# Causal attention with beacon tokens and a three-way maxout FFN on one core: the opening's loads, casts, masks and weight requests in another order

## The chip, the core and the metric

The kernel runs on one core of a Trainium2 chip. The core has a matrix engine (TensorE, "PE" in the profile, with its weight loads as "PEld"), VectorE ("DVE"), ScalarE ("ACT"), GpSimd ("POOL") and SyncE ("SP"), and 16 DMA engines that bring data from the chip's memory. Each engine runs its own list of instructions strictly in order, and waits at an instruction until what that instruction needs is there. The metric is the device time of one execution in microseconds. The program below is planned by hand: the order in which it is written is the order on each engine.

## The reference

Inputs are float32: `q`, `k`, `v` of shape 8 x 8 x 576 x 64 (batches, heads, tokens, width), 16 beacon keys and values for each head, three FFN matrices of 512 x 768 and one of 768 x 512.

```python
k_all = np.concatenate([beacon_k, k], axis=2)
v_all = np.concatenate([beacon_v, v], axis=2)
scores = scale * np.matmul(q, k_all.transpose(0, 1, 3, 2))
causal = np.zeros((S, Nb + S), dtype=bool)
causal[:, Nb:] = np.triu(np.ones((S, S), dtype=bool), k=1)
scores = np.where(causal, -1000000000.0, scores)
a = np.exp(scores - scores.max(-1, keepdims=True))
a /= a.sum(-1, keepdims=True) + 1e-09
attn = np.matmul(a, v_all)
x = attn.transpose(0, 2, 1, 3).reshape(B * S, H * D)
h = np.maximum(np.maximum(x @ w1, x @ w2), x @ w3)
out = h @ w_out
```

Every token sees the 16 beacons and the tokens up to itself. The output is 4608 x 512.

## The kernel before

**Units of work.** A *pair* is two heads of one batch; there are 32 pairs, four to a batch. For a pair, queries and keys are loaded in float32 (`load_pair`, L161), cast to bf16 (`cast_pair`, L192, with `cast_piece`, lines 181 and 186), turned on TensorE so that the head's width lies on partitions (`turn`, L297: `turn_apart` L337 early, `turn_pair` L344 later), and copied from the matrix engine's accumulators into `qT` and `kT` (L321, L332). The pair's beacon keys are copied into the first 16 columns of `kT` by `place_beacons` (L328). Then `emit_scores` (L375) makes the scores of a pair in four *groups* of key tiles (L385) and ScalarE takes their exponential (L394) into `at_sb`. `emit_masks` (L398) zeroes what lies above the diagonal: five small pieces for each pair, on VectorE by a product with a triangle (L408) for pairs 0 to 3, on GpSimd by a select (L410) for all later ones. `emit_pv` (L430) multiplies with a column of ones and with the values (L451), for a *quad* of two pairs and a half of the tokens at a time; `finish_pv` (L462) divides by the sums (L469, L471, L474) and writes `xT`.

**Values** of a batch come as five tiles of up to 128 tokens and all heads, in two pieces of three and two tiles (`load_v`, L199: DMA lines 208 and 213), and are cast by `cast_v` (L217, line 229). Neighbouring tiles with the same number of rows are cast by one instruction, so that tiles 1 and 2 go with tile 0. Values are read from memory in runs of 64 floats, 256 bytes; pairs from number 4 on in runs of 1536 bytes.

**FFN.** `mm1_unit` (L497) multiplies 512 tokens with one 128-column part of w1, w2 or w3, and VectorE keeps the maximum (L505, L507); `mm2_unit` (L514) does the output. The matrices are asked for on GpSimd's DMA queue (`load_w`, L238, two requests for each; `load_w_out`, L243), which casts on the way.

**Order.** `emit_all` (L671) goes through pairs `p` and steps `s`. Pairs 0 to 4 have four steps, one for each group ("fine" steps); later pairs have two. At a step TensorE gets the scores, then the work of `fine_at` (early turns, early value products, dummy products `keep_busy` that only keep the matrix engine occupied), then masks, then the value products of `pv_at`, then FFN units up to an allowance that grows with the steps, the next pair's turn, and what `plan` holds for that step. The value products of quad 2, the first of batch 1, stand at step (6, 0), behind that step's scores and ahead of its FFN units. The first FFN units stand at step (4, 3).

`plan` is filled by `at_step` (lines 618 to 638): casts on GpSimd and requests for weights. `C(...)` is a cast followed by `next_load()`, which issues the next entry of the list `loads` (lines 567 to 573) on SyncE's queue; `L(...)` is a call alone. SyncE's DMAs use eight semaphores in turn, so the ninth waits for the first to land, and a load into `st` waits for a free one of nine buffers. In the opening SyncE runs well ahead of what has been used.

Of the kernel before, what the change touches and what calls it, by code (L numbers as in the profile page):

```python
# [16 lines left out]
def kernel(  # L17
# [19 lines left out]
    d_model, d_ff = moe_w1.shape  # L37
# [19 lines left out]
    k_rows = [min(128, NK - 128 * t) for t in range(n_kt)]  # L57
# [9 lines left out]
    B_PE = 4  # L67
# [8 lines left out]
    NG = len(groups)  # L76
# [34 lines left out]
    bk16_1 = const.tile([NB_PE - Nb, H, D], BF16, name="bk16_1")  # L111
# [36 lines left out]
    by_pool = nc.gpsimd.tensor_copy  # L148
# [68 lines left out]
    def cast_v(b, piece, cast):  # L217
        st = stage.pop(("v", b, piece))
        if b not in v_tiles:
            v_tiles[b] = v_pool.tile([128, n_kt, H, D], BF16, name="v_sb")  # L220
        v_sb = v_tiles[b]
        t_lo, t_hi = V_PIECES[piece]
        t = t_lo
        while t < t_hi:
            t1 = t + 1
            while t1 < t_hi and k_rows[t1] == k_rows[t]:
                t1 += 1
            n = k_rows[t]
            cast(  # L229
                v_sb[0:n, t:t1].rearrange("p t h d -> p (t h d)"),  # L230
                st[0:n, (t - t_lo) * H * D : (t1 - t_lo) * H * D],
            )
            t = t1
# [92 lines left out]
    def place_beacons(p, copy):  # L326
        b, pi = divmod(p, PPB)
        copy(kTs[p % NT][:, 0:Nb], bT[:, pi, Nb * b : Nb * (b + 1)])  # L328
# [15 lines left out]
    def turn_pair(p, q_copy):  # L344
        banks = [pv_bank(i, [128, 1024], BF16) for i in range(2)]
        for i in range(2):
            turn(p, i, banks[i][:, 0:S])
        evac_q(p, banks[0][:, 0:S], q_copy)
        evac_k(p, banks[1][:, 0:S], by_dve)
# [25 lines left out]
    def emit_scores(p, gi):  # L375
        if gi == 0:
            at[p] = at_pool.tile([128, AT_W], BF16, name="at_sb")
        kT = kTs[p % NT]
        qT = qTs[p % NT]
        ps = sc_psum.tile([128, 2, 512], FP32, name="sc")  # L380
        off = 0
        for t, q0, q1 in groups[gi]:
            for e in range(2):
                hs = slice(64 * e, 64 * e + 64)
                nc.tensor.matmul(  # L385
                    ps[:, e, off : off + q1 - q0],
                    kT[hs, 128 * t : 128 * t + 128],
                    qT[hs, q0:q1],
                    start=True,
                    stop=True,  # L390
                    tile_position=(64 * e, 0),
                )
            off += q1 - q0
        nc.scalar.activation(  # L394
            out=both_heads(p, gi), in_=ps[:, :, 0 : g_width[gi]], func=AF.Exp, scale=scale
        )
# [146 lines left out]
    def emit_ffn(limit, pool=None, name="fps"):  # L543
        if done[0] + 1 <= limit and done[0] < len(units) and units[done[0]][0] <= ready[0]:
            _, fn, args = units[done[0]]
            fn(*args, pool or ffn_psum, name)
            done[0] += 1
            return True
        return False
# [5 lines left out]
    def at_step(p, g, *fns):  # L555
        plan.setdefault((p, g), []).extend(fns)

    def L(fn, *a):
        return lambda: fn(*a)

    def load_v_pieces(b):
        return [L(load_v, b, 0), L(load_v, b, 1)]

    def load_pairs(p0, p1):
        return [L(load_pair, p) for p in range(p0, p1)]

    loads = [L(load_pair, 0, nc.scalar), L(load_pair, 1, nc.scalar)] + load_pairs(2, 4)
    loads += [L(load_v, 0, 0), L(load_beacons, 1, B_PE, bk32_1), L(load_v, 0, 1)]
    loads += load_pairs(4, 5) + load_pairs(5, 6) + load_v_pieces(1) + load_pairs(6, 8)
    for b in range(2, B):  # L570
        if b == B_PE:
            loads.append(L(load_beacons, B_PE, B, bk32))
# [2 lines left out]
    def next_load(n=1):  # L575
        for _ in range(n):
            if loads:
                loads.pop(0)()

    def C(fn, *a):  # L580
        def run():
            fn(*a)
            next_load()

        return run

    def start():
        keep_busy(15)
        next_load()
        load_beacons(0, 1, bk32_0, nc.scalar)  # L590
        next_load(10)
        cast_piece(0, 0, by_dve)
        cast_piece(0, 1, by_act)
        stage.pop(("pair", 0))
        by_pool(bk16_0, bk32_0)
        next_load()
        q_ps = ffn_psum.tile([128, S], BF16, name="fps")
        k_ps = ffn_psum.tile([128, S], BF16, name="fps")
        turn(0, 0, q_ps)
        turn(0, 1, k_ps)  # L600
        evac_q(0, q_ps, by_act)
        evac_k(0, k_ps, by_dve)
        turn_beacons(0, 1, bk16_0)
        keep_busy(4)
        C(cast_pair, 1, by_pool, by_pool)()
# [9 lines left out]
    def steps(p):  # L615
        return [[gi] for gi in range(NG)] if p < P_FINE else [[0, 1], [2, 3]]

    at_step(0, 0, C(cast_pair, 2, by_pool, by_pool))
    at_step(0, 1, C(cast_pair, 3, by_pool, by_pool))
    at_step(1, 0, C(cast_v, 0, 0, by_pool))  # L620
    at_step(1, 1, C(cast_v, 0, 1, by_pool))
    at_step(1, 2, L(by_pool, bk16_1, bk32_1))
    at_step(1, 3, L(load_w, 0, 0, d_ff))
    at_step(2, 0, C(cast_pair, 4, by_pool, by_pool))
    at_step(2, 2, C(cast_pair, 5, by_pool, by_pool))
    at_step(3, 1, L(load_w, 1, 0, d_ff))
    at_step(3, 2, C(cast_v, 1, 0, by_pool))
    at_step(3, 3, C(cast_v, 1, 1, by_pool))
    at_step(4, 0, C(cast_pair, 6, by_pool, by_pool))
    at_step(4, 2, L(load_w, 2, 0, d_ff))  # L630
    at_step(4, 3, C(cast_pair, 7, by_pool, by_pool))
    at_step(5, 1, L(load_w_out))
    for p in range(8, B_PE * PPB):
        at_step(p - 2, 1, C(cast_pair, p, by_pool, by_pool))
    for b in range(2, B):
        p = b * PPB
# [7 lines left out]
        (0, 3): [L(turn_apart, 2, 1)],  # L644
        (1, 0): [L(turn_apart, 3, 0)],
        (1, 1): [L(turn_apart, 3, 1)],
        (1, 2): [L(keep_busy, 1, 256, True)],
        (1, 3): [L(keep_busy, 1, 256, True)],
        (2, 0): [L(emit_pv, 0, 0, 0, 2)],
        (2, 1): [L(emit_pv, 0, 0, 2, 4), finish_pv],  # L650
        (2, 2): [L(keep_busy, 1, 256, True)],
        (2, 3): [L(turn_beacons, 1, B_PE, bk16_1), L(keep_busy, 2, 256, True)],
        (3, 0): [L(turn_apart, 4, 0)],
        (3, 1): [L(turn_apart, 4, 1), L(emit_pv, 0, 1, 0, 2)],
        (3, 2): [L(emit_pv, 0, 1, 2, 4), finish_pv],
# [7 lines left out]
    for b in range(B_PE, B):  # L663
        p = b * PPB
# [6 lines left out]
    def emit_all():  # L671
        start()
        n_step = 0
        n_y = 0
        for p in range(NPAIR):
            b, pi = divmod(p, PPB)
            fine = p < P_FINE
            for s, gs in enumerate(steps(p)):
                for gi in gs:
                    emit_scores(p, gi)  # L680
                for fn in fine_at.pop((p, s), ()):
                    fn()
                for gi in gs:
                    emit_masks(p, gi, p < PPB)
                for args in pv_at.pop((p, s), ()):
                    emit_pv(*args)
                if fine:
                    allowed = 2 if (p, s) == (P_FINE - 1, NG - 1) else 0
                else:
                    n_step += 1  # L690
                    if n_step <= 9:
                        allowed = 2 + n_step * (UPB - 2) / 9
                    else:
                        allowed = (n_step - 1) * UPB / (2 * PPB)
                if not fine and s == 0 and p + 1 < B_PE * PPB:
                    place_beacons(p + 1, by_pool)
                emit_ffn(allowed)
                if not fine and s == 1 and p + 1 < B_PE * PPB:
                    turn_pair(p + 1, by_act)
                store_y(n_y)  # L700
                n_y = len(y_out)
                for fn in plan.pop((p, s), ()):
                    fn()
                emit_ffn(allowed)
                n_y = len(y_out)
                if not fine:
                    finish_pv()
                while emit_ffn(allowed):
                    pass
            if pi == 1 and b > 0:  # L710
                v_tiles.pop(b - 1)
        assert not plan and not loads and not pv_at
        for hf in range(2):
            emit_ffn(len(units))
            emit_ffn(len(units))
            emit_pv(NPAIR // 2 - 1, hf)
            finish_pv()
        store_y(len(y_out))
        alone[0] = True
        i = 0  # L720
        tail = [(ffn_psum, "fps"), (sc_psum, "sc")]
        while emit_ffn(len(units), *tail[i % 2]):
            i += 1
            store_y(len(y_out))

    with tc.manual_schedule():
        emit_all()
# [30 lines left out]
```

## Time and profile before

| What | Value |
|---|---|
| Five runs, median (lowest to highest) | 305.67 us (304.89 to 306.51) |
| The profiled execution, its own time | 303.82 us |
| Span of its instructions | 302.1 us |
| TensorE busy | 286.9 us, 95% of the span |
| VectorE, ScalarE, GpSimd busy | 174.5, 143.3, 127.1 us |
| Mean granted TensorE clock | 0.983 of full speed |
| Chain that ended last | TensorE 81%, DMA 6%, SyncE's queue 5%, GpSimd 2% |
| Landing of a pair's query load (288 KB), median | 5.3 us after its issue |
| Landing of a weight request (384 KB in bf16), median | 9.2 us after its issue |

The profile cuts the span into 40 slices and gives a busy tenth for each; "PEclk" is the share of full speed that TensorE was granted. An instruction group names its line in the kernel, the engine, and what it writes and reads (out<-in). A wait is put down to what ended it. "POOL v_sb L229 <- DMA st<-in_v_dram" reads: GpSimd, at the cast of values in line 229, waited for the load of values.

### The profile page before, as it was taken

The numbers are of one execution on the slowest core, as the hardware profiler recorded it, in microseconds if no ns is written. First come the engines' busy times: TensorE is split into PE (matmuls) and PEld (weight loads), VectorE is DVE, ScalarE is ACT, GpSimd is POOL, SyncE is SP. The second block draws the span as 40 slices with busy tenths as digits, with TensorE's granted clock in tenths as the row PEclk, the third lists the DMA queues.
The fourth block names the chain that finished last, engine by engine and source line by source line (L and its number), as shares of the span: only waits on it lengthen the run. The fifth ranks groups of instructions, "written<-read, shape, count | busy, mean of one in ns | idle before, by whom it ended". The sixth has DMA issues, their size and how long they took to land.

```text
span 302.1 us, 8614 instructions
## 1 busy us (share of the span) xinstructions
PE 286.9 (95%) x3560; PEld 148.9 (49%) x3560; DVE 174.5 (58%) x335; ACT 143.3 (47%) x220; POOL 127.1 (42%) x254
## 2 busy tenths in 40 slices
PE   7888849999999999999999999999999999999995
PEld 4545324554455555454445687545454544444442
DVE  2876525656666466646564656465736575275373
ACT  3877625573555464636463546455645531400300
POOL 3591594455667566455445544562243210000000
PEclk9959988999999999999999999999999999999999
DMA  7999999999699799999999998657402001102003
GB/s 262 220 225 213 230 252 247 215 242 213 181 308 205 221 262 235 175 194 266 283 202 182 258 263 143 119 142 197 101 36 106 2 0 72 72 0 112 28 2 139
DMA packets 83095, 51.55 MB, mean 171 GB/s; under 512 B 62064, under 2 KB 76656, under 8 KB 83056
## 3 DMA queue, kind: packets, MB, share of 16 engines
q1 hardware_dynamic: 80976, 47.23, 68.5%
q0 software_dynamic: 1648, 3.15, 5.5%
q8 instruction: 28, 0.46, 0.7%
q10 hardware_dynamic: 432, 0.62, 0.6%
q14 instruction: 11, 0.09, 0.1%
HBM read 35.13 MB, written 14.22 MB: 163 GB/s over the span
## 4 chain that ended last, share of the span: by engine, by line
PE 81%; DMA 6%; SPq 5%; POOL 2%; DVE 2%; issue 1%; ACT 0%; DVEq 0%
PE fps L497 41%; PE fps L514 13%; PE pv L451 11%; PE sc L385 8%; PE sc L497 5%; DMA st<-in_v_dram 4%; SPq L213 3%; PE sc L514 2%; DMA st<-in_q_dram 2%; PE pv L301 1%; SPq L249 1%; DVE kT L332 1%; POOL p L186 1%; POOL at_sb L410 1%; SPq L172 1%
## 5 line engine op out<-in xcount | busy, mean ns | idle before, releaser
L394 ACT ACTIVATE at_sb<-sc 128x992 bf16<-128x992 f32 (+3 forms) x128 | 103.6, 861 | 102.4 <-PE sc L385 102.2
L497 PE MATMUL fps<-xT,w_sb 128*128 128x512 bf16 (+1 forms) x648 | 140.2, 357 | 0.6 <-DVE xT L474 0.6
L497 PEld LDWEIGHTS <-w_sb 128*128 128x128 bf16 x720 | 65.8, 98 | 71.0 <-issue 14.9
L507 DVE TENSOR_TENSOR hT<-hT,fps 128x512 bf16<-128x512 bf16 x96 | 65.7, 685 | 45.3 <-PE fps L497 45.1
L410 POOL TENSOR_SCALAR_AFFINE_SELECT at_sb<-at_sb 128x256 bf16<-128x256 bf16 (+2 forms) x140 | 51.0, 383 | 95.8 <-ACT at_sb L394 94.4
L186 POOL CAST p<-st 96x768 bf16<-96x768 f32 x56 | 44.8, 827 | 2.6 <-DMA q_dram<-p 2.5
L514 PE MATMUL fps<-w_out_sb,hT 128*128 128x512 bf16 x180 | 41.8, 379 | 0.0
L385 PE MATMUL sc<-qT,kT 64*128 64x288 bf16 (+4 forms) x384 | 36.4, 288 | 4.5 <-POOL kT L328 3.4
L505 DVE CAST hT<-fps 128x512 bf16<-128x512 f32 x42 | 29.0, 690 | 19.9 <-PE fps L497 19.8
L522 DVE COPY y<-fps 128x512 f32<-128x512 f32 x30 | 20.7, 689 | 27.9 <-PE fps L514 27.9
L514 PEld LDWEIGHTS <-hT 128*128 128x128 bf16 x216 | 20.5, 98 | 25.0 <-DVE hT L507 1.3
L474 DVE TENSOR_TENSOR xT<-pv,recip 128x288 bf16<-128x288 f32 (+2 forms) x93 | 27.2, 348 | 6.2 <-ACT recip L471 4.4
L451 PE MATMUL pv<-at_sb,v_sb 128*32 128x192 bf16 (+4 forms) x1352 | 28.9, 232 | 0.0
L385 PEld LDWEIGHTS <-kT 64*128 64x128 bf16 x384 | 13.8, 95 | 29.4 <-issue 18.8
L229 POOL CAST v_sb<-st 128x1536 bf16<-128x1536 f32 (+2 forms) x24 | 21.5, 912 | 13.8 <-DMA st<-in_v_dram 13.7
L451 PEld LDWEIGHTS <-v_sb 128*32 128x32 bf16 (+1 forms) x1408 | 25.0, 98 | 2.6 <-issue 1.3
L451 PE MATMUL pv<-at_sb,ones 128*32 128x288 bf16 (+4 forms) x492 | 18.1, 263 | 1.4 <-DVE at_sb L408 0.8
L497 PE MATMUL sc<-xT,w_sb 128*128 128x512 bf16 x72 | 18.5, 379 | 0.0
L469 ACT ACTIVATE lnd<-pv 128x288 f32<-128x288 f32 x31 | 12.9, 416 | 5.8 <-PE pv L451 5.8
L451 PEld LDWEIGHTS <-ones 128*32 128x32 bf16 (+1 forms) x512 | 11.1, 97 | 8.8 <-issue 6.0
L507 DVE TENSOR_TENSOR hT<-hT,sc 128x512 bf16<-128x512 bf16 x12 | 8.2, 687 | 12.5 <-PE sc L497 12.3
L505 ACT CAST hT<-sc 128x512 bf16<-128x512 f32 x6 | 3.5, 585 | 23.7 <-PE sc L497 23.7
(47 smaller groups left out, 116.7 us busy)
## 6 DMA issues: line engine op xcount, KB each, us to landing
st<-in_q_dram SPq DMA_DIRECT2D x32, 288.0 KB, 5.3
out_dram<-y SPq DMA_DIRECT2D x36, 256.0 KB, 2.8
st<-in_k_dram SPq DMA_DIRECT2D x30, 288.0 KB, 5.5
st<-in_v_dram SPq DMA_DIRECT2D x24, 256.0 KB, 6.2
w_sb<-in_moe_w_dram POOLq DMA_DIRECT2D x6, 384.0 KB, 9.2
q_dram<-p SPq DMA_DIRECT2D x16, 144.0 KB, 2.5
k_dram<-p SPq DMA_DIRECT2D x16, 144.0 KB, 2.7
st<-in_v_dram SPq DMA_DIRECT2D x8, 224.0 KB, 6.1
```

The lines of the kernel that those rows point to most:

```text
L186: cast(t16.rearrange("p r h d -> p h r d"), st[0:QP, i * NQ2 : (i + 1) * NQ2].rearrange("p (h r d) -> p h r d", h=2, r=QR),)
L229: cast(v_sb[0:n, t:t1].rearrange("p t h d -> p (t h d)"), st[0:n, (t - t_lo) * H * D : (t1 - t_lo) * H * D],)
L385: nc.tensor.matmul(ps[:, e, off : off + q1 - q0], kT[hs, 128 * t : 128 * t + 128], qT[hs, q0:q1], start=True, stop=True, tile_position=(64 ...
L394: nc.scalar.activation(out=both_heads(p, gi), in_=ps[:, :, 0 : g_width[gi]], func=AF.Exp, scale=scale)
L410: nc.gpsimd.affine_select(out=view, in_=view, compare_op=ALU.is_ge, fill=0.0, base=x0, pattern=[[0, 2], [1, hi - lo]], channel_multiplier=-1,)
L451: nc.tensor.matmul(ps[bank][32 * j : 32 * j + 32, lo + q0 - qa : lo + qb - qa], lhsT, at_view(PPQ * quad + j // 2, t, j % 2, q0, qb), star ...
L474: nc.vector.tensor_mul(xT[:, 2 * g + part - 1, c0 + ca : c0 + cb], ps[bank][:, lo : lo + cb - ca], recip[:, ca:cb],)
L497: nc.tensor.matmul(ps[:, o0 : o0 + n], w_in[i][:, ct, 128 * ft : 128 * (ft + 1)], xT[:, ct, x0 : x0 + n], start=(ct == 0), stop=(ct == n_c ...
L505: (by_act if alone[0] else by_dve)(hT[:, ft, :], ps)
L507: nc.vector.tensor_max(hT[:, ft, :], hT[:, ft, :], ps)
L514: nc.tensor.matmul(ps, hT[:, ft, 128 * tt : 128 * (tt + 1)], w_out_sb[:, ft, :], start=(ft == 0), stop=(ft == n_ft - 1),)
L522: nc.vector.tensor_copy(y, ps)
```

## The change

The value casts of batch 0 are made for each tile alone. Pair 6 is loaded ahead of batch 1's values. Pair 0's masks are taken from VectorE and put on GpSimd, behind the casts of pairs 1 to 3 and ahead of the first values' casts. Pair 4's casts go ahead of the first weight request, pair 6's ahead of the second; batch 1's value casts, pair 7's casts and the requests for the third and the output matrix move to later steps. Four calls of dummy products get two products of 320 columns in place of one or two of 256.

```diff
@@ cast_v
-            while t1 < t_hi and k_rows[t1] == k_rows[t]:
+            while b > 0 and t1 < t_hi and k_rows[t1] == k_rows[t]:
@@ loads
-    loads += load_pairs(4, 5) + load_pairs(5, 6) + load_v_pieces(1) + load_pairs(6, 8)
+    loads += load_pairs(4, 7) + load_v_pieces(1) + load_pairs(7, 8)
@@ plan
     at_step(0, 1, C(cast_pair, 3, by_pool, by_pool))
+    at_step(1, 0, *[L(emit_masks, 0, gi) for gi in range(NG)])
     at_step(1, 0, C(cast_v, 0, 0, by_pool))
     at_step(1, 1, C(cast_v, 0, 1, by_pool))
     at_step(1, 2, L(by_pool, bk16_1, bk32_1))
-    at_step(1, 3, L(load_w, 0, 0, d_ff))
-    at_step(2, 0, C(cast_pair, 4, by_pool, by_pool))
+    at_step(1, 3, C(cast_pair, 4, by_pool, by_pool))
+    at_step(2, 0, L(load_w, 0, 0, d_ff))
     at_step(2, 2, C(cast_pair, 5, by_pool, by_pool))
-    at_step(3, 1, L(load_w, 1, 0, d_ff))
-    at_step(3, 2, C(cast_v, 1, 0, by_pool))
-    at_step(3, 3, C(cast_v, 1, 1, by_pool))
-    at_step(4, 0, C(cast_pair, 6, by_pool, by_pool))
-    at_step(4, 2, L(load_w, 2, 0, d_ff))
-    at_step(4, 3, C(cast_pair, 7, by_pool, by_pool))
-    at_step(5, 1, L(load_w_out))
+    at_step(3, 2, C(cast_pair, 6, by_pool, by_pool))
+    at_step(3, 3, L(load_w, 1, 0, d_ff))
+    at_step(4, 1, C(cast_v, 1, 0, by_pool))
+    at_step(4, 2, C(cast_v, 1, 1, by_pool))
+    at_step(5, 0, L(load_w, 2, 0, d_ff))
+    at_step(5, 0, C(cast_pair, 7, by_pool, by_pool))
+    at_step(6, 0, L(load_w_out))
@@ fine_at
-        (1, 2): [L(keep_busy, 1, 256, True)],
-        (1, 3): [L(keep_busy, 1, 256, True)],
+        (1, 2): [L(keep_busy, 2, 320, True)],
+        (1, 3): [L(keep_busy, 2, 320, True)],
-        (2, 2): [L(keep_busy, 1, 256, True)],
-        (2, 3): [L(turn_beacons, 1, B_PE, bk16_1), L(keep_busy, 2, 256, True)],
+        (2, 2): [L(keep_busy, 2, 320, True)],
+        (2, 3): [L(turn_beacons, 1, B_PE, bk16_1), L(keep_busy, 2, 320, True)],
@@ emit_all
-                for gi in gs:
+                for gi in gs if p > 0 else ():
                     emit_masks(p, gi, p < PPB)
```

On GpSimd the list around step (6, 0) is now: first three of pair 4's masks, values of batch 1 (first piece), a mask, values (second piece), pair 4's last mask, pair 5's first three masks, pair 6's beacons, third weights, casts of pair 7, pair 5's last two masks.

## The prediction
> **What bounds the kernel now.** I read the page's slices first, because the change touches only the opening.
>
> ```profile
> PE   7888849999999999999999999999999999999995
> POOL 3591594455667566455445544562243210000000
> PEclk9959988999999999999999999999999999999999
> DMA  7999999999699799999999998657402001102003
> ```
>
> A slice is 7.55 us. From slice 7 (about 53 us) TensorE is 90% busy or more at full clock, in an order fixed by the program: whatever is won or lost before that moves the end by as much, and nothing later has room to give it back. The dips are slice 3 (clock) and slices 5 and 6 (TensorE idle, then clock). The DMA row is full throughout: the opening is a queue for bytes. The waits of the first 50 us name the dip in slice 5:
>
> ```profile
> POOL v_sb L229 <- DMA st<-in_v_dram: 13.7, 3, 9.9
> PE sc L385 <- POOL kT L328: 3.4, 1, 3.4
> ```
>
> The columns are total, times and longest. TensorE waits once, for 3.42 us, for a 16-column copy on POOL that was ready long before; POOL itself had waited 9.91 us for batch 1's values. The timeline from 31 us shows what stood between:
>
> ```profile
> 33.80 2.71 POOL L229 CAST v_sb<-st 128x1536 bf16<-128x1536 f32 x3 [9.91 <-DMA st<-in_v_dram]
> ...
> 37.16 1.58 POOL L186 CAST p<-st 96x768 bf16<-96x768 f32 x2
> ...
> 39.33 1.08 POOL L238 DMA_DIRECT2D w_sb<-in_moe_w_dram  x2
> ...
> 40.76 1.60 POOL L186 CAST p<-st 96x768 bf16<-96x768 f32 x2
> ...
> 42.31 1.01 POOL L410 TENSOR_SCALAR_AFFINE_SELECT at_sb<-at_sb 128x224 bf16<-128x224 bf16 x3
> ...
> 43.27 0.19 POOL L328 COPY kT<-bT 128x16 bf16<-128x16 bf16 x1
> 43.41 0.75 POOL L410 TENSOR_SCALAR_AFFINE_SELECT at_sb<-at_sb 128x256 bf16<-128x256 bf16 x2
> 43.51 0.74 PE L385 MATMUL sc<-qT,kT 64*128 64x288 bf16 x8 [3.42 <-POOL kT L328]
> ...
> 44.19 0.62 PE L451 MATMUL pv<-at_sb,ones 128*32 128x288 bf16 x12
> ```
>
> Columns: start, length, work. From 33.80 POOL never rests. Two things follow one another on it: pair 6's beacons at 43.27 release the scores of step (6, 0), and pair 5's last mask, done at 44.17, releases the value products at 44.19. TensorE had finished everything else at 40.10, and 1.23 us of that were waits for POOL's cast of pair 6 (0.89 + 0.34), so it could have been there at 38.9. **The stage is bound by DMA, then by POOL, with some 5 us of slack on TensorE.** Why batch 1's values came late is in the trace's packets: from 23 to 31 us the weights' queue moved about 30 packets of 3 KB in each 0.5 us and the load queue about as many of 256 B. Turns are by packet, so the values got under a tenth of the bytes until two weight matrices were in.
>
> **The change, part by part.** Working forward in the profiled execution (303.82 us, span 302.1).
>
> *Masks of pair 0 to POOL.* DVE loses five multiplies of 0.23 to 0.28 us, 1.3 us. POOL gains five selects of 0.32 to 0.40 (rows at 42.31 and 43.41), 1.8 us, from 10.7 to 12.5, where it idled 3.40 us for the values. The Trainium skill speaks against such a move (SBUF — State Buffer, "Who interferes with whom": a GpSimd instruction holds the port pair that it shares with VectorE to its end). The row: DVE's 16-column copy takes 0.15 us alone and 1.08 at 14.50, beside POOL's 1.47 us cast; but DVE's 576-column copies take 0.74 to 0.76 beside POOL or not. By the row the move wins DVE 1.3 us; by the rule up to 0.4 is lost at each of the two such copies in that stretch, leaving 0.5. I take 1.0. *Values of batch 0 tile by tile:* the same port; three casts of 0.61 (row 35.34) for one of 1.47, tile 0 usable 0.9 us sooner, 0.36 us more POOL work beside waits for loads. All this brings step (2, 0) forward by about a microsecond. It is worth **0** at the end: the slack above hides it. Without that cover it would be worth that microsecond.
>
> *More dummy columns.* 1280 more, at 512 in 0.216 us 0.54 us at full clock, 1.08 at half, on TensorE before 20 us; hidden too. What they are worth hangs on the clock. The trace grants 0.5 from 16.41 to 23.24. The skill (TensorE: Matmul & The Clock Gate, "What's actually happening") lets the clock fall after a window of about 3.4 us of idleness. The row disagrees: the window before the fall, 13.00 to 16.41, was 2.28 us busy (67%), its longest gap 0.83 us. By the rule the dummies do nothing there; by the row (67% fell, 79% at 23.24 did not) going to about 76%, and more with the shorter wait at (2, 0), probably keeps full clock and wins up to 3.4 us of TensorE before 24 us. Either way step (3, 0) then waits for pair 4's load (landed 18.21 and 19.42, both kernels), and slack hides the rest: **0**.
>
> *First weights later.* POOL casts pair 4 first. q 18.25 to 19.07, k 19.45 to 20.27; then two requests, 1.2 us, instead of from 18.13: 2.1 us later. They landed at 26.56 and 28.60, so now about 28.7 and 30.8. The first FFN matmul stood at 31.53: 0.7 us left, and 3 us more of slack behind it. **0**; if the second half came at 32, TensorE would reach (6, 0) at 39.4, still early.
>
> *Loads: pair 6 ahead of batch 1's values.* SP's queue is the same up to pair 5 (landed 21.79). Pair 6 (two of 288 KB at 1.18 us) lands at 23.0 and 24.2. POOL casts pair 5 (21.5 to 23.1) and pair 6 (to 25.0), then asks for weights 2 at 25.0 instead of 22.83. First weight packet came 4.45 us after the first request, so weights 1 run 24.7 to 28.9, weights 2 from 29.5 to 33.7 (four took 8.4 us). Values of batch 1 start at 22.65 in packets, run alone for 2 us (0.41 MB), crawl under each matrix (0.08 MB each), get the gap (0.13 to 0.33), and have 0.3 to 0.5 of 1.21 MB left at 33.7. At 0.21 MB per us that is 36 to 37.
>
> A second count checks it: when the last value tile lands, the same loads are in as before when pair 6's keys landed, 37.73 (pairs 0 to 6, two batches of values, weights 1 and 2). The DMA share of 34 to 36 us was 0.68, 0.6 us idle. So the last tile lands between 37.1 and 37.7: **37.4**.
>
> *POOL behind it.* Casts of pair 6, 1.55 us, are gone from this stretch, and so is the mask work that had queued: it fits in the waits before. What is left after 37.4, start to start from the trace: last tile 0.57, pair 4's last mask 0.36, pair 5's first three 0.96, beacons 0.14, weights 3 1.08, pair 7 1.55 (loaded by 40), pair 5's last two 0.76: 5.42. Scores of (6, 0) go at 39.4 instead of 43.51, but the value products behind them on TensorE, and every FFN matmul behind those, wait for the last mask: **37.4 + 5.4 = 42.8 instead of 44.19: −1.35 us**. The wait thus moves from the beacons to the masks. Weights 3 are asked for at 39.4 as before (39.33), weights out about 1 us later; they had 7 us to spare (landed 57.12, first used 64.3).
>
> *Clock after the wait.* Before: half clock from 43.72 to 47.13, 1.7 us lost. Now TensorE idles about 0.6 us, scores for 0.55, and idles again for 2.8. By the skill's rule a fall needs a whole idle window, so it may not fall, −1.7; by the row (a 67% window fell) it falls as before, 0. I take 0.
>
> Sum: −1.35 us on 303.82, that is 302.5. The five runs have a median of 305.67, 1.85 above the profiled execution; I carry the difference over: **304.3 us**. From no change a measurement here can tell about 0.3%, 0.9 us.
>
> **Rivals.**
>
> - *Nothing to be seen* (27%). The bytes ahead of (6, 0) are the same ones in another order, and weights 3 and pair 7's casts still stand ahead of the masks. For it: POOL's chain is only 1.35 us shorter and a last tile at 38.0 instead of 37.4 leaves 0.7. Against: 1.55 us of casts really leave the stretch. Time 305.7, within 0.9.
> - *Slower: the values starve behind both weight matrices* (22%). Pair 6 now takes the 2.4 us that the values had before the weights' packets came. If the first weight packet comes earlier than 24.7, or weights 2 follow without a gap and late (latency 5.4 us was seen for the third: asked 39.33, first packet 44.7), 0.8 MB is left at 34.6: 3.8 us, plus 1.3 from packet to landing, gives 39.8, and 5.4 of POOL makes 45.2: 1.0 us late, plus 0.5 for a longer cold clock: 307.2. It decides from a last tile at 38.7 on. For it: 256 B packets against 3 KB. Against: the second count.
> - *The clock stays up as well* (10%): −1.35 −1.7, with the last tile at 36.8 another −0.6: 302.0. For it: the idle time is now cut in two by the scores. Against: slice 3, where a lighter lull was enough.
>
> **How the numbers follow.** The forecast case, last tile between 36.5 and 37.8, has 41% and gives 303.4 to 304.7. With the 302.0 case faster has 51%; a small part of the forecast (last tile near 37.8) falls to the same side as the second rival, 27%; slower 22%. The range leaves out about a tenth at each end: 302.4 to 306.8.
>
> **What would show it.** Right: POOL's cast at L229 for batch 1 starts near 35 and its last tile near 37.4; TensorE's long wait is at L451 on a POOL mask and not at L385; pair 6's transposes at L301 wait for nothing; weights 1 land near 30.8. The steps at 0 are right if slice 3's clock changes and the start of (6, 0)'s value products does not follow it. Wrong: values of batch 1 landing after 38.7; a wait at the first L497 for weights 1 beyond 34; or value products starting where POOL was long done.

## The result, and the profile after

The changed kernel takes 303.48 us (median of 32 runs, 301.55 to 305.54); the kernel before took 304.85 us in the 55 runs made beside it. The ratio is **0.9947, 95% interval 0.9932 to 0.9962**: about 0.5% faster, 1.6 us (the two medians differ by 1.4). Forecast was a gain of 1.35 us. The profiled execution took 303.02 us with a span of 301.3 (before: 303.82 and 302.1).

The same four rows of the page's slices:

```profile
PE   7796859999999999999999999999999999999995
POOL 3875294455666583555455544652243210000000
PEclk9989998999999999999999999999999999999999
DMA  7999999999699999989998999586302001102003
```

Slices are counted from 0 here. TensorE's deepest dip is still slice 5, and it is milder, 5 tenths for 4. From slice 6 on its row is the same. The early dip of the clock, in slice 2 (the "slice 3" of the forecast), is milder too, 8 tenths for 5, and slice 3 is less busy than before. The waits of the first 50 us (total, times, longest):

```profile
POOL v_sb L229 <- DMA st<-in_v_dram: 9.7, 4, 6.9
...
PE pv L451 <- POOL at_sb L410: 2.1, 1, 2.1
...
PE sc L385 <- POOL kT L328: 1.2, 1, 1.2
```

One wait of 3.4 us for the beacons has become two: 1.2 us for the beacons and 2.1 us for a mask. What GpSimd does in between is in the timeline of GpSimd and, for the two lines of PE, of TensorE:

```profile
35.70 1.46 POOL L229 CAST v_sb<-st 128x1536 bf16<-128x1536 f32 x1 [6.93 <-DMA st<-in_v_dram]
37.11 0.41 POOL L410 TENSOR_SCALAR_AFFINE_SELECT at_sb<-at_sb 128x256 bf16<-128x256 bf16 x1
37.46 1.16 POOL L229 CAST v_sb<-st 128x512 bf16<-128x512 f32 x2
38.58 1.37 POOL L410 TENSOR_SCALAR_AFFINE_SELECT at_sb<-at_sb 128x256 bf16<-128x256 bf16 x4
39.90 0.19 POOL L328 COPY kT<-bT 128x16 bf16<-128x16 bf16 x1
40.03 1.08 POOL L238 DMA_DIRECT2D w_sb<-in_moe_w_dram  x2
41.10 1.61 POOL L186 CAST p<-st 96x768 bf16<-96x768 f32 x2
42.65 1.72 POOL L410 TENSOR_SCALAR_AFFINE_SELECT at_sb<-at_sb 128x256 bf16<-128x256 bf16 x5
...
40.15 0.54 PE L385 MATMUL sc<-qT,kT 64*128 64x288 bf16 x8 [1.16 <-POOL kT L328]
...
43.11 0.55 PE L451 MATMUL pv<-at_sb,ones 128*32 128x176 bf16 x6 [2.11 <-POOL at_sb L410]
```

The chain on GpSimd is the one that was forecast: values land and are cast, then masks, beacons, third weights, pair 7 and the last masks. Six value products run early; the rest start at 43.11, where before all of them started at 44.19. Pair 6's casts, 1.58 us of the old chain, are no longer in it. The values landed at 35.55 (third tile) and 37.51 (last).

### The profile page after: what moved, and what is told of

The parts are those of the page before. It is cut to its first block, busy times and chain, and to the rows that moved or that the text cites. A ratio compares the mean times of both kernels' runs of the same rounds, so it can differ in the third digit from the quotient of the medians.

```text
span 301.3 us, 8622 instructions
## 1 busy us (share of the span) xinstructions
PE 285.6 (95%) x3563; PEld 148.0 (49%) x3563; DVE 175.0 (58%) x330; ACT 143.3 (48%) x220; POOL 128.6 (43%) x261
## 4 chain that ended last, share of the span: by engine, by line
PE 81%; DMA 9%; POOL 3%; SPq 2%; DVE 2%; issue 1%; ACT 0%; POOLq 0%; DVEq 0%
PE fps L497 41%; PE fps L514 13%; PE pv L451 11%; PE sc L385 8%; DMA st<-in_v_dram 5%; PE sc L497 5%; PE sc L514 2%; DMA st<-in_q_dram 2%; DMA st<-in_k_dram 2%; SPq L213 1%; DVE kT L332 1%; POOL at_sb L410 1%; POOL v_sb L229 1%; PE pv L301 1%; POOL p L186 1%
## 5 line engine op out<-in xcount | busy, mean ns | idle before, releaser
L410 POOL TENSOR_SCALAR_AFFINE_SELECT at_sb<-at_sb 128x256 bf16<-128x256 bf16 (+2 forms) x145 | 52.7, 384 | 99.2 <-ACT at_sb L394 97.7
L385 PE MATMUL sc<-qT,kT 64*128 64x288 bf16 (+4 forms) x384 | 36.1, 286 | 3.2 <-POOL kT L328 1.2
L451 PE MATMUL pv<-at_sb,v_sb 128*32 128x192 bf16 (+4 forms) x1352 | 28.4, 229 | 0.6 <-issue 0.6
L385 PEld LDWEIGHTS <-kT 64*128 64x128 bf16 x384 | 13.7, 94 | 28.9 <-issue 20.4
L451 PEld LDWEIGHTS <-v_sb 128*32 128x32 bf16 (+1 forms) x1408 | 24.5, 96 | 3.9 <-issue 2.8
L229 POOL CAST v_sb<-st 128x512 bf16<-128x512 f32 (+2 forms) x26 | 21.4, 839 | 9.7 <-DMA st<-in_v_dram 9.7
L451 PE MATMUL pv<-at_sb,ones 128*32 128x288 bf16 (+4 forms) x492 | 17.5, 258 | 2.2 <-POOL at_sb L410 2.1
L451 PEld LDWEIGHTS <-ones 128*32 128x32 bf16 (+1 forms) x512 | 10.9, 96 | 9.3 <-issue 7.4
L507 DVE TENSOR_TENSOR hT<-hT,sc 128x512 bf16<-128x512 bf16 x12 | 8.2, 687 | 12.5 <-PE sc L497 12.2
```

Of the source, the lines that this page charges most:

```text
L229: cast(v_sb[0:n, t:t1].rearrange("p t h d -> p (t h d)"), st[0:n, (t - t_lo) * H * D : (t1 - t_lo) * H * D],)
L385: nc.tensor.matmul(ps[:, e, off : off + q1 - q0], kT[hs, 128 * t : 128 * t + 128], qT[hs, q0:q1], start=True, stop=True, tile_position=(64 ...
L410: nc.gpsimd.affine_select(out=view, in_=view, compare_op=ALU.is_ge, fill=0.0, base=x0, pattern=[[0, 2], [1, hi - lo]], channel_multiplier=-1,)
L451: nc.tensor.matmul(ps[bank][32 * j : 32 * j + 32, lo + q0 - qa : lo + qb - qa], lhsT, at_view(PPQ * quad + j // 2, t, j % 2, q0, qb), star ...
L507: nc.vector.tensor_max(hT[:, ft, :], hT[:, ft, :], ps)
```

## The experiments

Two theories at the start. **A**: the gain is GpSimd's shorter chain ahead of quad 2's value products, and all that the change does before 20 us is hidden. **B**: the gain is the faster start (masks off VectorE, tile casts, dummies). A third, **C**, came up on the way: part of the loss is the clock that falls after the wait. In the table, "release" is the start on TensorE of the value products behind their last wait in the profiled execution. "Half clock" is the mean time in a run at half of TensorE's clock, from each run's granted clock and span: 2 x (1 − clock) x span, as the traces grant either all or half. For the kernel before it was 13.4 us in the 43 runs beside e1 to e4, 15.2 us beside e5 to e9 and 13.0 us beside e10 to e12.

| Kernel | Ratio to before (95%) | Last value tile lands | Release | Half clock |
|---|---|---|---|---|
| Kernel before | 1 | 35.65 | 44.19, no wait | 13.0 to 15.2 us |
| Changed kernel | 0.9947 (0.9932 to 0.9962) | 37.51 | 43.11 | 8.3 us |
| e1 order only | 0.9964 (0.9945 to 0.9983) | 37.76 | 43.78 | 13.1 us |
| e2 start only | 1.0002 (0.9985 to 1.0020) | 35.88 | 45.46, no wait | 11.3 us |
| e3 pair 7 behind the masks | 0.9878 (0.9841 to 0.9916) | 38.64 | 42.27 | 5.3 us |
| e4 second weights later | 0.9897 (0.9854 to 0.9940) | 37.95 | 43.10 | 6.9 us |
| e5 values before weights | 0.9941 (0.9922 to 0.9960) | 34.36 | 39.6, no wait | 9.0 us |
| e7 masks on VectorE | 0.9952 (0.9933 to 0.9972) | 38.00 | 43.66 | 9.0 us |
| e8 second weights in halves | 0.9980 (0.9961 to 0.9999) | 39.09 | 44.28 | 9.5 us |
| e9 old dummies | 0.9969 (0.9955 to 0.9982) | 39.06 | 44.30 | 13.5 us |
| e10 dummies in the wait | 0.9916 (0.9888 to 0.9944) | 37.80 | 43.14 | 6.1 us |
| e11 both moves | 0.9866 (0.9832 to 0.9899) | 36.86 | 40.50 | 4.4 us |
| e12 pair 7 and dummies | 0.9885 (0.9857 to 0.9912) | 38.70 | 42.22, no wait | 7.8 us |

"No wait" means that the products follow what stands ahead of them on TensorE; before and in e2 these are the scores, which had waited 3.42 us for the beacons. One profiled execution per kernel stands behind the landings, and they scatter: seven kernels with the same loads and weights in the same order up to the last tile (the changed kernel, e1, e3, e7, e9, e10, e12) have it at 37.51 to 39.06. Distances within one execution are therefore the safer reading: release minus last tile is 5.6 us in the changed kernel, 5.1 to 6.0 in e1, e4, e7, e8, e9 and e10.

**The change in two halves (e1, e2).** e1 is the kernel before with the new `loads` and `plan` and nothing else; e2 the other half:

```diff
# e1, against the changed kernel
-            while b > 0 and t1 < t_hi and k_rows[t1] == k_rows[t]:
+            while t1 < t_hi and k_rows[t1] == k_rows[t]:
-    at_step(1, 0, *[L(emit_masks, 0, gi) for gi in range(NG)])
-                for gi in gs if p > 0 else ():
+                for gi in gs:
...
# and keep_busy as before; e2 has these lines as changed, loads and plan as before
```

> Before, with the change's order of loads, casts and weight requests alone; pair 0's masks stay on VectorE, batch 0's values are cast in one piece, the dummy products are as before. Theory A (the gain is GpSimd's shorter chain ahead of quad 2's value products): ratio to before 0.994 to 0.996, the value products of step (6, 0) released between 42.8 and 43.6 us. Theory B (the gain is the faster start: masks, tile casts, dummies): ratio 1.000, within 0.002.

> Before, with the other half alone: pair 0's masks on GpSimd, batch 0's values cast tile by tile, more dummy products; loads, casts and weight requests in the old order. Theory A: ratio 1.000, within 0.002, value products of step (6, 0) at 44.2 us as before, whatever the clock does near 15 us. Theory B: ratio 0.994 to 0.996.

The order alone gives 0.9964 and a release at 43.78, both just beyond what A named; the start alone gives 1.0002. B falls. In e2 the release was at 45.46 and not at 44.2 as A named: pair 6's keys landed at 39.07 in that execution, against 37.73 in the one of the kernel before, and GpSimd waited 1.12 us for them. That the two halves do not quite add up to 0.9947 is within the intervals, and is taken up at e9. Which move inside the new order carries the gain was not tried move by move.

**Pair 7's casts behind the masks (e3).** This takes the one block out of GpSimd's chain that the value products do not need:

```diff
-    at_step(5, 0, C(cast_pair, 7, by_pool, by_pool))
+    at_step(5, 1, C(cast_pair, 7, by_pool, by_pool))
```

> The changed kernel, with pair 7's two casts moved on GpSimd from ahead of pair 5's last two masks to behind them. Theory A: those casts are 1.55 us of the chain, so the value products are released near 41.6 instead of 43.1, and the time is 1.2 to 1.7 us below the changed kernel's: ratio to before 0.989 to 0.991. Theory B: no change against the changed kernel, 0.994 to 0.996. A third possibility: the third weight matrix (landed at 52.4, first needed at 54.4) becomes the wait, and less than half of it is won.

0.9878: more than A named, though its interval takes in A's range. TensorE's timeline of e3:

```profile
40.84 0.54 PE L385 MATMUL sc<-qT,kT 64*128 64x288 bf16 x8 [1.10 <-POOL kT L328]
...
42.27 0.55 PE L451 MATMUL pv<-at_sb,ones 128*32 128x176 bf16 x6 [0.58 <-POOL at_sb L410]
```

The release is 3.6 us behind the last tile instead of 5.6: A's 1.55 us and a little. The second wait shrank from 2.11 to 0.58 us. In this execution the clock did not fall behind it, which A had not counted. The third weights (landed 52.60) did not become a wait.

**Second weights later (e4).**

```diff
-    at_step(3, 3, L(load_w, 1, 0, d_ff))
+    at_step(4, 1, L(load_w, 1, 0, d_ff))
```

> The changed kernel, with the second weight matrix asked for after pair 4's first three masks (near 28.8 us) instead of at 25.6. Theory A with turns by packet: batch 1's values have the load queue to themselves for 3 to 4 us more, the last tile lands at 33.5 to 35.5 instead of 37.5, the value products are released 2 to 3.5 us earlier, ratio to before 0.984 to 0.988. Rival (only the bytes ahead of the values count, and the values' short packets cost the same with and without weights beside them): last tile within 1 us of 37.5, ratio 0.993 to 0.996. Rival: the second weights come too late and TensorE waits at L497 for them, ratio above 0.994.

A miss for A. The third tile did land sooner, at 33.17, but the last at 37.95, where the first rival had it: the second weights came while it was still out. GpSimd waited 2.31 us for it, and the release was at 43.10 as in the changed kernel. The time came out lower all the same (301.55 us, though the ends of the two intervals overlap), and that goes with the clock, which stayed up behind this wait in the profiled execution.

**Values ahead of both matrices (e5).** Against the changed kernel:

```diff
-    at_step(3, 3, L(load_w, 1, 0, d_ff))
     at_step(4, 1, C(cast_v, 1, 0, by_pool))
+    at_step(4, 1, L(load_w, 1, 0, d_ff))
     at_step(4, 2, C(cast_v, 1, 1, by_pool))
-    at_step(5, 0, L(load_w, 2, 0, d_ff))
-    at_step(5, 0, C(cast_pair, 7, by_pool, by_pool))
+    at_step(4, 2, L(load_w, 2, 0, d_ff))
+    at_step(5, 1, C(cast_pair, 7, by_pool, by_pool))
```

> The changed kernel, with the second weights asked for after the first piece of batch 1's values is cast, the third after the second piece, and pair 7's casts behind pair 5's last masks. Theory A: no weights run beside batch 1's values after the first matrix, the last tile lands at 34 to 35.5 us, pair 5's last mask is done by 40, the value products of (6, 0) start when TensorE comes to them (39.5 to 41), and the clock does not fall there. Ratio to before 0.980 to 0.986. Rival: the second weights (expected to land near 41 to 42) or pair 7, now beside two matrices, become the next wait: a wait at the seventh unit of L497 or at L301 of step (6, 1), ratio 0.986 to 0.992.

The rival had the wait right; the ratio, 0.9941, is above even its range. TensorE's timeline:

```profile
39.12 0.55 PE L385 MATMUL sc<-qT,kT 64*128 64x288 bf16 x8 [0.16 <-DVE kT L332]
...
41.73 0.61 PE L497 MATMUL fps<-xT,w_sb 128*128 128x512 bf16 x2 [1.28 <-DMA w_sb<-in_moe_w_dram]
44.25 2.74 PE L497 MATMUL fps<-xT,w_sb 128*128 128x512 bf16 x6 [1.91 <-DMA w_sb<-in_moe_w_dram]
```

TensorE no longer waits for GpSimd at this step. The second matrix, asked for at 33.03 behind pairs 7 to 9 in the load queue, landed at 41.68 and 44.20, and the 3.2 us waited for it ate what was won. The clock fell behind them, from 44.24. The wait moved on from GpSimd's chain to the weights, and the ratio is that of the changed kernel.

**The start's parts (e7, e9).** e7 puts pair 0's masks back on VectorE, e9 the old dummies back, both in the changed kernel.

```diff
# e7
-    at_step(1, 0, *[L(emit_masks, 0, gi) for gi in range(NG)])
-                for gi in gs if p > 0 else ():
+                for gi in gs:
# e9, and likewise at (1, 3), (2, 2) and (2, 3)
-        (1, 2): [L(keep_busy, 2, 320, True)],
+        (1, 2): [L(keep_busy, 1, 256, True)],
```

> The changed kernel with pair 0's masks back on VectorE. In the changed kernel's trace two 16-column copies on VectorE took 0.69 and 1.55 us beside GpSimd's masks and casts instead of 0.15, so the move won 1.3 us of VectorE and lost 1.9. Theory A: the 1.55 us copy shrinks to 0.2 to 0.7 us, and nothing of it reaches the end: ratio to before 0.993 to 0.997, as the changed kernel. Theory B, weakened by the run of the start alone: above 0.997.

> The changed kernel with the dummy products as before. Theory A: the clock near 15 to 25 us falls as often or longer, hidden by the wait for GpSimd: ratio to before 0.993 to 0.997. Rival: the dummies keep the clock and are worth more than 0.2% of the changed kernel's gain: ratio above 0.9975.

e7 is at the changed kernel's ratio, and the long copy on VectorE shrank from 1.55 to 0.30 us: the masks' place is worth nothing that these runs can tell. e9 is at the upper edge of A's range. Against the changed kernel half clock rose from 8.3 to 13.5 us, and the ratio from 0.9947 to 0.9969. The intervals overlap, so that the dummies' 0.2% is likely and not shown. Two other kernels point the same way: e1, with the old dummies too, at 13.1 us of half clock, and e7, with the new ones and run beside e9, at 9.0 us and a median of 303.33 us against 304.19.

**Smaller weight packets (e8).**

```diff
-    at_step(3, 3, L(load_w, 1, 0, d_ff))
+    at_step(3, 3, L(load_w, 1, 0, FH), L(load_w, 1, FH, d_ff))
```

> The changed kernel with the second matrix asked for in two column halves, so that a weight packet has 768 bytes and not 3072. Turns by packet: the values' 256 bytes get a quarter of the bytes beside these weights and not a twelfth, the first three tiles land 1 to 3 us sooner than 35.5 and the last at 35.5 to 37.3, the second matrix lands 1 to 3 us later than 34.7; ratio to before 0.988 to 0.994. If turns go by bytes or the load queue has no right to a turn: landings within 0.5 us of the changed kernel's, ratio 0.993 to 0.997.

The expectation of turns by packet failed: third tile 35.22, last tile 39.09 (changed kernel: 35.55 and 37.51), second matrix 36.49 instead of 34.73. The DMA packets that began in one microsecond in which both queues were full, counted in the two traces:

```
                              weights               values
changed kernel, 30.5 to 31.5   66 packets, 203 KB    54 packets, 14 KB
e8, 32.5 to 33.5              248 packets, 178 KB    73 packets, 18 KB
```

In the changed kernel it looked like one packet for one packet; with short weight packets it is one value packet to more than three weight packets. In the time of the DMA engines the values got about a tenth of what the weights got either way (0.10 us to 1.02, 0.14 us to 1.16). The short packets made the weights take longer: 10.7 us from the first request for the second matrix to its landing, against 9.1 to 9.6 in the changed kernel, e3, e7, e9, e10 and e12. That the last tile came later for it is not shown: e9, with long packets, has it at 39.06.

**Dummies in the wait (e10).** To part the clock from the chain, twelve dummy products were put between the scores and the value products of step (6, 0):

```diff
         (4, 1): [L(emit_pv, 1, 1, 0, 4, True), finish_pv],
+        (6, 0): [L(keep_busy, 12, 320, True)],
```

> The changed kernel with twelve dummy products of 320 columns (1.6 us at full clock) behind the scores of step (6, 0), in the wait for pair 5's last masks. The release of the value products does not move (43 us in the changed kernel), only the clock can. Theory C (part of the loss is the clock that falls after this wait): the clock stays up behind 43 us, 1 to 1.7 us less than the changed kernel, ratio to before 0.989 to 0.992. Theory A alone (the chain is all): ratio 0.993 to 0.996.

The release is the same, 43.14 against 43.11, and the ratio is 0.9916. TensorE's timeline behind the release in the changed kernel:

```profile
43.47 0.65 PE L451 MATMUL pv<-at_sb,v_sb 128*32 128x288 bf16 x32
44.05 3.08 PE L497 MATMUL fps<-xT,w_sb 128*128 128x512 bf16 x8
```

and in e10:

```profile
40.64 1.80 PE L354 MATMUL fps<-busy 128*128 128x320 bf16 x12
...
43.50 0.65 PE L451 MATMUL pv<-at_sb,v_sb 128*32 128x288 bf16 x32
44.08 1.90 PE L497 MATMUL fps<-xT,w_sb 128*128 128x512 bf16 x7
```

The same eight FFN products (one record is missing in e10's trace) took 3.08 us, most of them at half clock, and 1.90 at full. Step (6, 1) begins 1.15 us sooner, at 45.91 instead of 47.06, and step (7, 0) 1.47 us sooner, at 49.02 instead of 50.49. So C stands beside A: the 1.5 us is plain in the trace. Over many runs it comes to some 0.3% (0.9916 against 0.9947), and there the two intervals overlap a little, so that its size over runs is likely and not settled.

**Both moves (e11), and pair 7's move with dummies (e12).** e11 is e3's and e4's edit in one kernel; e12 is e3 with `(6, 0): [L(keep_busy, 4, 320, True)]`.

> The changed kernel with both moves that won: pair 7's casts behind pair 5's last masks, and the second weights asked for after pair 4's first three masks. If the last tile of the values (38.0 in the one, 38.6 in the other) is what counts, the release is near 3.6 us behind it, 41.5 to 42.3, and the time that of pair 7's move alone: ratio 0.986 to 0.989. If their gains add (1.5 and 2.1 us below the changed kernel): 0.981 to 0.984.

> Pair 7's casts behind pair 5's last masks, and four dummy products in the short wait that is left (0.6 us). The release stays 3.6 us behind the last tile. If the clock was still falling in some executions after that wait, they are rarer: ratio 0.985 to 0.989. If not, the same as without dummies, 0.988, or 0.2 us above where the dummies are longer than the wait.

e11 is the fastest kernel here: 300.51 us, ratio 0.9866. Its release is 3.6 us behind the last tile again, 40.50 behind 36.86, and its waits are down to 0.43 and 0.59 us. The ratio is the one named for the case that the last tile counts and the gains do not add. Its interval reaches over e3's; that it beats the changed kernel (0.9947) is clear, that it beats e3 is not. e12 is at e3's ratio (0.9885 and 0.9878): once the wait is short, dummies in it bring nothing that six runs can tell.

## Why the prediction was right, and where its steps were off

**Right in place and sign; the size is near in part by luck.** The place was step (6, 0): the longer wait moved from L385 to L451 and to a mask, as forecast, and pair 6's transposes waited for nothing. The two halves (e1, e2) show the order of loads and casts as the carrier, and e3 shows by taking one block out that this chain sets the time. The gain of 1.6 us stands against 1.35 forecast, but the forecast put all of it on the chain and 0 on the clock. The two kernels with the new order and the old dummies, e1 and e9, gained 1.1 and 0.9 us with half clock as long as before; the rest of the 1.6 goes with the shorter half clock. The intervals overlap, so this split is likely and not settled.

- *Landings.* Forecast 37.4 for the last tile, 28.7 and 30.8 for the first weights, 29.5 for the second weights' first packet; measured 37.51, 28.43 and 30.46, 29.78. The count of bytes held; that it held to 0.1 us is luck, as the same order of loads had its last tile as late as 39.06 (e9), and pair 6's keys, on which the second count rests, moved by 1.3 us between two executions of the old order.
- *What released the value products before.* My reading, pair 5's last mask, is not what the rows show. The mask was done at 44.16, but the products stand behind the scores, which ended at 44.26 by the model, and show no wait. Scores and mask were done at nearly the same time, so the sum suffers little.
- *GpSimd behind the last tile.* Forecast 5.4 us, last mask at 42.8; measured 5.9 to that mask's end near 43.4, the first products behind the one before it at 43.11. The missing half microsecond is a term that I left out: the last tile's cast stood behind the first piece's 1.46 us cast, a mask and the fourth tile's, which ended later than the landing alone would have allowed.
- *The slower rival.* It was to decide from a last tile after 38.7 on; the changed kernel's came at 37.51. The limit was too sharp: e9 had 39.06 and a release at 44.30, and was still faster than the kernel before over its runs (0.9969). Under the weights the values did crawl (14 KB per us), but they had their two microseconds before, and some 0.3 MB between the matrices, as counted. (The third matrix's first packet, which I read at 44.7, came at 44.94; nothing in the sum rests on it.)
- *Turns by packet.* The reading behind "under a tenth of the bytes" was wrong as a rule (e8): with shorter weight packets the queues did not take turns one packet each. The share itself, taken from the trace of the same pair of loads, was right, and so the sum was.
- *Clock after the wait: 0.* As a difference between the two kernels' profiles this held: it fell in both (43.72 to 47.13 before, 44.62 to 48.03 now). The 3.41 us ahead of the second fall were busy for 41%, so the reading by the row was right. A later restart of the clock gave back 0.3 us of the 1.08 us won at the release: 0.8 us of profile against profile. Over many runs the changed kernel is at half clock for less time, 8.3 us. e10 shows what this term is worth, 1.5 us in one execution and some 0.3% over runs (the intervals overlap a little); I had held it for a rival of 10%.
- *Dummies: 0, and probably full clock near 15 us.* The clock still fell, from 13.90 to 17.31, one stretch of 3.41 us instead of two. In the old order all of the start was worth nothing (e2, 1.0002). In the new order the dummies may be worth 0.2% (e9). The cover is thinner than the 5 us I named: in e1 TensorE came to (6, 0) at 40.27, and waited 0.56 us for the beacons and 2.10 us for the mask.
- *Masks to GpSimd: +1.0 us for VectorE.* Too high. VectorE's timeline in the changed kernel, the three 16-column copies:

```profile
9.86 0.69 DVE L328 COPY kT<-bT 128x16 bf16<-128x16 bf16 x1
...
11.80 1.55 DVE L328 COPY kT<-bT 128x16 bf16<-128x16 bf16 x1
...
14.98 0.15 DVE L328 COPY kT<-bT 128x16 bf16<-128x16 bf16 x1
```

and in the kernel before, two of pair 0's masks and the third copy:

```profile
9.22 0.95 DVE L408 TENSOR_TENSOR at_sb<-at_sb,tri 128x224 bf16<-128x224 bf16 x2
...
14.50 1.08 DVE L328 COPY kT<-bT 128x16 bf16<-128x16 bf16 x1
```

In the changed kernel the three copies took 2.39 us together; before they took 0.15, 0.15 and 1.08, 1.38 in all. So 1.0 us was given back here. The masks' 1.3 us was not read rightly either: one of the five had lasted 0.74 us, from 9.42 to 10.16, beside GpSimd's casts. What is left can be seen at the third copy, which ended at 15.13 instead of 15.58: 0.45 us. That copy did shrink from 1.08 to 0.15, as forecast of the tile casts. But the first copy now stood beside GpSimd's cast of pair 3, which ended at 10.5, and the second beside a mask (to 12.2) and then two casts (to 13.3). The rule of the Trainium skill (SBUF — State Buffer, "Who interferes with whom": whichever of VectorE and GpSimd comes first has the shared ports for its whole instruction) was nearer to the truth here than what I read from the row, but the second copy lasted over several of GpSimd's instructions, not to the end of one. All of it was hidden (e7). e7's own expectation was too simple as well: its "lost 1.9" left out that the old 1.08 us copy was gone.

## What to carry to other kernels

Where an in-order engine feeds the bound one, ask of each instruction ahead of the release whether that release needs it: moving one pair of casts behind the masks (e3) brought about as much again as the whole change. A wait on TensorE can have a second price, the slow clock behind it. Measure that apart, with dummies in the wait, before looking for it in the chain; in the traces with a short wait (e3, e11) it was gone without them. When a load is moved ahead of another under a full DMA queue, name what is asked for next and when it must be there: in e5 the release came 3.5 us sooner, and 3.2 us of it went into waits for the next matrix.

## What the runs showed of the hardware that was not expected

- From a weight request on GpSimd to its first packet it took 4.2 us (changed kernel, 20.33 to 24.52) and 5.2 us (e5, 33.03 to 38.26) where the load queue ahead held runs of 1536 bytes, and 1.3 us (e4, 31.07 to 32.38) where it held the values' runs of 256 bytes. The requests are alike; why it differs was not tried.
- The clock's fall does not follow one threshold of TensorE's busy time. In the profile of the kernel before, the 3.41 us up to 16.41 were busy for 67% and it fell; those from 36.89 to 40.31 were busy for 58% and it did not. In the changed kernel it fell after 57% (up to 13.90) and not after 54% (27.55 to 30.97). Leaving out the transposes does not mend it: 66% and 37% in the kernel before. Its two stretches (busy time by engine with counts, granted clock, DMA share and GB/s):

```profile
13.00:16.41 3.41, 2.28 (x40) 1.04 (x34) 3.41 (x10) 2.84 (x4) 1.93 (x2) 1.00 0.91 191
...
36.89:40.31 3.42, 1.97 (x18) 0.85 (x16) 1.63 (x3) 1.38 (x3) 3.42 (x7) 1.00 1.05 258
```

- At step (6, 0) the length of TensorE's waits does part the thirteen profiles. With the waits for other engines and for loads at this step added up, the clock fell in the seven with 2.7 us or more (before and e2 3.4, the changed kernel 3.3, e1 2.7, e5 3.2, e8 and e9 3.9), and stayed up in the six with 2.0 us or less (e3 and e4 1.7, e7 2.0, e10 and e12 1.6, e11 1.0). In e8 it fell at 41.33, behind the first 2.3 us of its waits. This is a count; only e10 changed the idle time and left the release in its place.
- A 16-column copy on VectorE of 0.15 us took up to 1.55 us beside GpSimd's masks and casts.
